# Chunk-selected attention and a squared-ReLU layer on one core: the last two sequences score two heads at once, and the chunk selection becomes a mask spread by DMA

## The chip, the cores and the metric

The kernel runs on one core of a Trainium2 chip. A core has five engines with instruction streams of their own: TensorE (PE in the profile; its weight loads are listed as PEld), VectorE (DVE), ScalarE (ACT), GpSimd (POOL) and SyncE (SP, which here only issues DMAs). They meet through semaphores. Data lies in SBUF (128 partitions), matmuls write to PSUM (eight banks of 512 floats per partition), and 16 DMA engines move data to and from DRAM. The metric is the device time of one execution in microseconds.

## The reference

Four sequences of 768 positions, eight heads of 64 dimensions. Keys are cut into 24 chunks of 32. For each query, an upper bound of its score against each chunk is worked out from the chunk's smallest and largest key; the six chunks with the highest bound are kept, future chunks being barred, and the query attends to the earlier positions of the kept chunks alone. The result goes through a layer with a squared ReLU.

```python
k_min, k_max = k_chunks.min(axis=3), k_chunks.max(axis=3)
ub = sum(maximum(q * k_min, q * k_max), axis=-1)        # 24 bounds a query
ub = where(pos // 32 >= chunk, ub, -1e9)
top_chunks = argsort(ub)[..., -6:]
scores = where(chunk_of_j in top_chunks and j <= i, q @ k.T / 8, -1e9)
attn = exp(scores - max) / (sum(...) + 1e-9)
x = (attn @ v) reordered to [3072, 512]
out = (relu(x @ w_in) ** 2) @ w_out                     # 512 -> 2048 -> 512
```

## The kernel before, in words

Work is cut into 16 head pairs (four a sequence, `p` from 0 to 15; `hh` is the head in the pair). The first 128 positions of each sequence see at most four chunks and are treated apart (`first_attention`, line 566); the rest is five query tiles of 128 positions per head.

For each pair, `stage_a` (line 622) prepares the operands. Keys and queries of sequences 0 and 1 are turned on TensorE; those of sequences 2 and 3 (`BY_DMA = 2`) come already turned from DMA transposes on SP's queue (tiles `kt`, `qt`, two heads on 2 x 64 partitions). VectorE reduces each chunk to its maximum and minimum (line 697), TensorE makes the bounds (660, 662), VectorE adds the bar on future chunks (722), finds the eight highest (668) and marks the chunks that are not among the six (727). The marks are turned (on TensorE, or for sequences 2 and 3 by DMA, line 389) and copied below the queries as 24 more rows (682). Keys are copied likewise above 24 rows of -32768 at the chunk's own columns (694, 336). So one matmul over 64 + 24 = 88 rows gives a score and takes 32768 off wherever the chunk is not chosen: nothing else has to know the selection.

`stage_b` (766) makes, for each head, five PSUM banks of four 128x128 score tiles (`BANKS`, 748; line 782), the exponential of each bank on ScalarE (804), the triangle on the diagonal tiles on VectorE or GpSimd (`causal`, 756), and the products with the values (793). VectorE divides by the sums (612, 614). `ffn` (823) turns the result by DMA or TensorE and runs the up-projection (866), ReLU (873, 875), square (884) and down-projection (897), one call for the first tiles and one for each sequence.

The order is not that of the code. Every piece is an operation with engines and costs, a due time, needs and buffers; `Plan.order` (115) simulates the engines and DMA queues once on the host and takes, on the engine that can start first, the operation with the earliest due time. The instructions are then written in that fixed order. The dictionary `P` (240) holds the due times' parameters. Buffers are slots by tag: three PSUM banks "ps", one "tp", two "av", two "ff"; six "e" tiles for exponentials; six "kq" tiles for natural or turned keys and queries. Loads are DMAs on GpSimd's queue (all of them in a fixed order), output stores and DMA transposes go through SP's queue.

## Time and profile before

| what | value |
|---|---|
| median of 3 runs | 266.53 us (265.86 to 267.04) |
| profiled execution, span from first to last instruction | 263.6 us |
| TensorE busy | 251.4 us, 95% |
| ScalarE busy | 197.8 us, 75% |
| VectorE busy | 183.0 us, 69% |
| GpSimd busy | 106.4 us, 40% |
| score matmuls (line 782) | 51.7 us busy, 320 instructions |
| exponentials (line 804) | 86.4 us busy, 160 instructions |
| DMA | 26.51 MB, mean 101 GB/s |

The page has a row of 40 equal slices per engine, each digit the busy tenths of 6.6 us. Groups of instructions are listed as "line engine operation output<-input shape xcount | busy us, mean ns of one | idle before, and what ended it". Matmuls are pipelined: one has a duration of some 0.2 us, but the next can start long before it ends, so the pace is read from start to start.

### The profile page before, as it was taken

How to read it: one execution, taken by the hardware profiler on the slowest of the kernel's cores; microseconds unless marked ns; L12 is line 12 of the kernel's file. 1: busy time of each engine (PE TensorE's matmuls, PEld its weight loads, DVE VectorE, ACT ScalarE, POOL GpSimd, SP SyncE). 2: the span in 40 equal slices, each digit the busy share in tenths (PEclk: the TensorE clock that was granted, in tenths of full speed). 3: DMA queues.
4: the chain of work that ended last, by engine and by line, in shares of the span. 5: the costliest groups of instructions: out<-in, count | busy, mean ns of one | idle time of the engine just before them, and what ended most of it. 6: DMA issues, size and time to landing. Idle time of an engine off the chain costs nothing.

```text
span 263.6 us, 6555 instructions
## 1 busy us (share of the span) xinstructions
PE 251.4 (95%) x2382; PEld 164.1 (62%) x2405; DVE 183.0 (69%) x663; ACT 197.8 (75%) x395; POOL 106.4 (40%) x185
## 2 busy tenths in 40 slices
PE   6899999999999999999999999998999999999995
PEld 1577566666687666665686645666865564765443
DVE  7569999778999999998999943644757142455000
ACT  6658897859899999999989845987866692677111
POOL 7998987799555599833311201110200010000000
PEclk9799999999999999999999999999999999999999
DMA  8999999999999999995440001154000113400122
GB/s 153 156 175 180 181 198 190 94 126 174 170 151 166 149 157 143 123 145 148 87 93 15 2 20 75 44 82 101 2 0 15 42 44 99 120 2 0 40 82 80
DMA packets 106336, 26.51 MB, mean 101 GB/s; under 512 B 99008, under 2 KB 103360, under 8 KB 106304
## 3 DMA queue, kind: packets, MB, share of 16 engines
q0 software_dynamic: 75088, 13.11, 67.9%
q1 hardware_dynamic: 31216, 12.98, 24.0%
q8 instruction: 19, 0.31, 0.5%
q14 instruction: 13, 0.11, 0.2%
HBM read 27.26 MB, written 6.29 MB: 127 GB/s over the span
## 4 chain that ended last, share of the span: by engine, by line
PE 62%; DVE 24%; ACT 8%; issue 3%; DMA 2%; SPq 0%; ACTq 0%; DVEq 0%
PE py L897 25%; PE ph L866 20%; PE ps L782 8%; PE av L793 4%; DVE h L884 4%; DVE kr L697 4%; DVE m L668 3%; DVE qsc L283 3%; ACT e L804 2%; DMA xT<-x 2%; ACT ht L873 2%; DVE x L614 2%; ACT qsc L281 2%; DVE kqc L283 1%; DVE ubm L722 1%
## 5 line engine op out<-in xcount | busy, mean ns | idle before, releaser
L866 PE MATMUL ph<-xT,w_in_sb 128*128 128x256 bf16 (+2 forms) x592 | 95.7, 304 | 1.6 <-DMA xT<-x 1.2
L804 ACT ACTIVATE e<-ps 128x512 bf16<-128x512 f32 x160 | 86.4, 608 | 7.5 <-PE ps L782 4.4
L897 PE MATMUL py<-w_out_sb,h 128*128 128x512 bf16 (+2 forms) x377 | 87.9, 370 | 1.2
L762 POOL TENSOR_SCALAR_AFFINE_SELECT e<-e 128x128 bf16<-128x128 bf16 (+1 forms) x88 | 31.0, 365 | 101.0 <-ACT e L804 89.1
L866 PEld LDWEIGHTS <-w_in_sb 128*128 128x128 bf16 x592 | 55.6, 97 | 24.9 <-DMA xT<-x 1.6
L873 ACT ACTIVATE ht<-ph 128x384 bf16<-128x384 f32 (+2 forms) x130 | 58.9, 457 | 16.2 <-PE ph L866 12.5
L884 DVE TENSOR_TENSOR h<-ht 128x256 bf16<-128x256 bf16 (+2 forms) x148 | 47.8, 333 | 16.4 <-ACT ht L873 12.9
L897 PEld LDWEIGHTS <-h 128*128 128x128 bf16 x400 | 36.2, 97 | 33.8
L782 PE MATMUL ps<-qsc,kqc 88*128 88x128 bf16 (+1 forms) x320 | 51.7, 272 | 0.3 <-DVE ubm L722 0.2
L782 PEld LDWEIGHTS <-kqc 88*128 88x128 bf16 x320 | 27.6, 97 | 14.8 <-issue 0.8
L281 ACT COPY ob<-py 128x512 f32<-128x512 f32 (+2 forms) x22 | 12.5, 570 | 29.2 <-PE py L897 29.1
L793 PEld LDWEIGHTS <-e 128*128 128x128 bf16 x640 | 29.6, 97 | 6.4 <-issue 0.3
L793 PE MATMUL av<-vn,e 128*128 128x65 bf16 x480 | 29.6, 193 | 0.0
L759 DVE TENSOR_TENSOR e<-e,tri 128x128 bf16<-128x128 bf16 (+1 forms) x40 | 9.7, 242 | 14.9 <-ACT e L804 14.2
L614 DVE TENSOR_TENSOR x<-av,rc 128x320 bf16<-128x320 f32 (+1 forms) x40 | 18.7, 472 | 0.5
L668 DVE MAX8 m<-ubm 128x8 f32<-128x24 f32 x160 | 15.5, 167 | 0.0
L697 DVE TENSOR_REDUCE kr<-kT 128x24 bf16<-128x768 bf16 x16 | 14.8, 951 | 0.2
L697 DVE TENSOR_REDUCE kr<-kt 128x24 bf16<-128x768 bf16 x16 | 14.8, 935 | 0.0
L793 PE MATMUL av<-v,e 128*128 128x65 bf16 x160 | 13.9, 193 | 0.1
L875 DVE TENSOR_SCALAR ht<-ph 128x256 bf16<-128x256 f32 (+2 forms) x18 | 8.2, 454 | 8.2 <-PE ph L866 8.2
L612 DVE RECIPROCAL rc<-av 128x5 f32<-128x5 f32 (+1 forms) x40 | 7.2, 184 | 9.4 <-PE av L793 8.5
L281 ACT COPY qsc<-sT 24x256 bf16<-24x256 bf16 (+1 forms) x29 | 12.4, 427 | 1.6 <-DMA sT<-selb 0.9
(92 smaller groups left out, 258.7 us busy)
## 6 DMA issues: line engine op xcount, KB each, us to landing
out_dram<-ob SPq DMA_DIRECT2D x23, 256.0 KB, 2.2
w_in_sb<-in_moe_w_in_dram POOLq DMA_DIRECT2D x4, 512.0 KB, 7.2
w_out_sb<-in_moe_w_out_dram POOLq DMA_DIRECT2D x4, 512.0 KB, 8.8
vn<-in_v_dram POOLq DMA_DIRECT2D x15, 128.0 KB, 6.9
nt<-in_k_dram POOLq DMA_DIRECT2D x10, 128.0 KB, 6.6
nt<-in_q_dram POOLq DMA_DIRECT2D x10, 128.0 KB, 5.3
kn<-in_k_dram POOLq DMA_DIRECT2D x8, 80.0 KB, 7.0
qn<-in_q_dram POOLq DMA_DIRECT2D x8, 80.0 KB, 5.7
```

The lines of the kernel that those rows point to most:

```text
L281: nc.scalar.copy(dst, src)
L614: return plan.op({"DVE": 0.06 + 0.00108 * D * n}, due, lambda _: nc.vector.tensor_mul(x(), av[:, :, 0:D], rc[:, 0:n].unsqueeze(2).to_broad ...
L668: nc.vector.max(out=m8[:, i, hh], in_=ubm[:, i, hh])
L697: nc.vector.tensor_reduce(kr[:, mm].rearrange("d (t c) -> d t c", c=128 // CH) if b >= BY_DMA else kr[:, mm], part(kT).rearrange("d t (c j ...
L762: nc.gpsimd.affine_select(out=e, in_=e, compare_op=ALU.is_ge, fill=0.0, base=0, channel_multiplier=-1, pattern=[[0, n], [1, 128]])
L782: nc.tensor.matmul(ps[:, 128 * c:128 * (c + nt)], lhsT=kqs[:, s, hh, 128 * j:128 * (j + 1)], rhs=qss[:, s, hh, 128 * (t0 - 1):128 * (t0 - ...
L793: nc.tensor.matmul(av[:, t - 1], lhsT=e[:, 128 * c:128 * (c + 1)], rhs=value_tile(b, h, j), start=(i == 0 and c == 0), stop=(i == len(BANK ...
L804: nc.scalar.activation(e.tile, ps.tile, ACT.Exp, scale=scale), [sc], [ps, e])
L866: nc.tensor.matmul(ph.tile, lhsT=w_in_sb[:, ki, 128 * f:128 * (f + 1)], rhs=xT[:, c0 // 128:c1 // 128, ki], start=(ki == 0), stop=(ki == N ...
L873: nc.scalar.activation(ht.tile, ph.tile, ACT.Relu)
L884: {"DVE": 0.067 + w / 1920}, at[0] + P["h2"], lambda _: nc.vector.tensor_mul(h2[f][:, c0:c1], ht.tile, ht.tile), [op], [ht, h2[f]])))
L897: nc.tensor.matmul(py.tile, lhsT=h2[f][:, 128 * t:128 * (t + 1)], rhs=w_out_sb[:, f, c0:c1], start=(f == 0), stop=(f == NFI - 1))
```

## The change

Sequences 0 and 1 stay as they are, in `stage_a` and `stage_b`. For sequences 2 and 3 two new functions take over.

`stage_a_turned` makes bounds and the eight highest as before, then marks the chosen chunks (four comparisons, only for chunks up to the tile's own), multiplies the marks by 3e38, turns them by a DMA transpose and stores them to a DRAM tile `seen`. Four DMAs on GpSimd's queue then read `seen` so that each row, 512 bytes for both heads of the pair, lands in the 32 partitions of its chunk: a tile `mask` of 128 partitions x 21 key-and-query tiles x 2 heads x 128 queries. GpSimd zeroes the triangle in the five diagonal tiles of the mask. No 88-row operands are built: the copies of keys, queries and marks are gone for these sequences.

`score_banks` computes the scores from the turned keys and queries themselves: for each 128x128 tile, a matmul of head 0 on rows 0 to 63 and one of head 1 on rows 64 to 127, by turns, into two banks. Two such steps, four banks (three "ps" and "tp"), make one operation. `stage_b_turned` takes the exponential, then the minimum with the mask on VectorE (0 where a key is not seen, 3e38 where it is), then the values.

The masks share a tag "set" of three slots with the 88-row sets of sequences 0 and 1 (two slots) and the natural keys and queries of sequence 1 (one). "e" goes from six to eight, "kq" from six to four; the bounds of these sequences go to "ff". The planner gets a cost `SWITCH` when TensorE passes between operations of 128 and of 64 rows, and all parameters in `P` are new, among them 59 single shifts of due times.

```diff
+    SWITCH = 0.095
...
+                if op.rows != rows:
+                    cost += self.SWITCH
+                rows = op.rows
...
-    P = dict(lead=[0, 207.45, 109.14, 153.29, -29.2, 112.12, 38.49, 53.35, 112.23, 30.95,
...
-             sel=2, loads='Q3 K3 V0 V1 Q2 K2 i0 V2 k0 V3 q0 i1 k1 v2 q1 i2 '
...
+    P = dict(lead=[-41.26, 277.74, 117.47, 192.23, -33.04, 156.27, 37.46, 53.28,
...
+             h2=-5.788, later='q1 k1 v1 k2 v3 q2 k3 v2 q3', shift={1035: 18.86, 381:
...
+             xt=(1, 2, 3), ub='ff', tp=1, vm2=4.275, va2=52.931,
...
-    plan = Plan({"tp": 1, "ps": 3, "av": 2, "ff": 2, "e": 6, "h2": NFI + 6, "ht": 3,
-                 "ob": 3, "kq": 6, "nt": 6,
+    plan = Plan({"tp": 1, "ps": 3, "av": 2, "ff": 2, "e": 8, "h2": NFI + 6, "ht": 3,
+                 "ob": 3, "kq": 4, "nt": 6, "set": 3, "seen": 3,
...
-    kqs = consts.tile([KC, NSET, 2, S], BF16, tag="kqs", name="kqc")
-    qss = consts.tile([KC, NSET, 2, QC], BF16, tag="qss", name="qsc")
+    sets = [buffer("set", [128, 2, 2, S + QC], name="kqc") for _ in range(2)]
+
+    def kqs(rows, s, *cols):
+        return sets[s // 2][(rows, s % 2, *cols, slice(0, S))]
+
+    def qss(rows, s, *cols):
+        return sets[s // 2][(rows, s % 2, *cols, slice(S, S + QC))]
...
+        both = buffer("set", [128, 2, NS, H, D], name="kqn")
         for nm in "kq":
-            if b < BY_DMA:
+            if b == BY_DMA - 1:
+                nat[nm, b] = both
...
+    UNITS = [(t, j) for t in range(1, NT) for j in range(t + 1)]
+    NU = len(UNITS)
+    FIRST = [UNITS.index((t, 0)) for t in range(1, NT)]
+    BIG = 3.0e38
+    NM = NU + 1
+    NB = NU // 4
+    PLACE = {(t, j): j + (0, 0, 3, 6, 10, 15)[t] for t, j in UNITS}
+    masks = {}
+    written = []
+
+    def stage_a_turned(p):
+        b, hp = divmod(p, NP)
+        s = p % NSET
+        t0 = HALVES * p - P["lead"][p]
+        op = plan.op
+        kT, qT = turned["k", b], turned["q", b]
+        qp, qm = buffer("qp", [128, QC]), buffer("qm", [128, QC])
+        ub = buffer(P["ub"], [128, NS, 2, NC], F32, name="ub")
+        sT = buffer("st", [128, 2, 128], name="sT")
+        seen = buffer("seen", [2 * 128, 128], name="seen")
+        mask = masks[p] = buffer("set", [128, NM, 2, 128], name="mask")
+
+        def like(t):
+            return t.rearrange("d (t u j) -> d u t j", u=2, j=64)
+
+        kb = chunk_bounds(
+            p, t0, list(loaded["k", b]), kT, lambda t: t[:, :, hp],
+            lambda t: t.rearrange("d t (c j) -> d t c j", j=CH),
+            lambda t: t.rearrange("d (t c) -> d t c", c=128 // CH))
+        sq = halves(qp, qm, lambda: qT[:, :, hp].rearrange("d t (u j) -> d u t j", u=2),
+                    like, list(loaded["q", b]), qT, t0, 0.34)
+        ubm, m8, m = ranked(p, t0, sq, kb, qp, qm, ub)
+        chosen = selbs[:, s].rearrange("p t h c -> p (t h c)")[:, 0:2 * 128]
+
+        def select(i0, i1):
+            n = 4 * (i1 + 1)
+            c0 = 8 * PLACE[i0 + 1, 0]
+            nc.vector.tensor_tensor(
+                chosen[:, c0:c0 + 2 * n * (i1 - i0)].rearrange(
+                    "p (i c h) -> p i h c", h=2, c=n), ubm[:, i0:i1, :, 0:n],
+                m8[:, i0:i1, :, TOPK - 1:TOPK].to_broadcast([128, i1 - i0, 2, n]),
+                op=ALU.is_ge)
+
+        def pick(*runs):
+            for r in runs:
+                select(*r)
+
+        def enlarge():
+            nc.vector.tensor_single_scalar(chosen[:, 0:8 * NM], chosen[:, 0:8 * NM], BIG,
+                                           op=ALU.mult)
+
+        sel = [op({"DVE": 0.23}, t0 + 19, lambda _: pick((0, 2), (2, 3)),
+                  m[:1] + prepared.get((p - NSET, "sT"), []), [ubm, m8])]
+        sel = [op({"DVE": 0.37}, t0 + 19, lambda _: (pick((3, 4), (4, 5)), enlarge()),
+                  m + sel, [ubm, m8])]
+        t = turn_by_dma(lambda: sT.tile, lambda: chosen, t0 + 21, sel, [sT],
+                        640, -0.8)
+        prepared[p, "sT"] = [t]
+        w = op({"SP": 0.45}, t0 + 23, lambda _: nc.sync.dma_start(
+            out=seen.tile.rearrange("(x r) j -> r x j", r=128), in_=sT.tile),
+            [t] + written[-1:], [sT, seen, mask], packets=300, turns=True, late=1.0)
+        written.append(w)
+
+        def spread_rows(g):
+            rows = seen[0:8 * NM].rearrange("(u g h) j -> g u (h j)", g=4, h=2)
+            nc.gpsimd.dma_start(
+                out=mask[32 * g:32 * g + 32].rearrange("c u h j -> c u (h j)"),
+                in_=rows[g].unsqueeze(0).to_broadcast([32, NM, 2 * 128]))
+
+        spread = [op({"POOL": 0.86}, t0 + 25 + g, lambda _, g=g: spread_rows(g),
+                     [w], [seen, mask], packets=1850, free=True, late=0.2)
+                  for g in range(4)]
+        for i in range(NB):
+            u = [PLACE[x] for x in UNITS[4 * i:4 * i + 4] if x[0] == x[1]][0]
+            prepared[p, "mask", i] = [op(
+                {"POOL": 0.37}, t0 + 30 + i, lambda _, u=u: causal("POOL", mask[:, u], 2),
+                spread, [mask])]
...
+    bursts = {}
+
+    def bank(p, hh, i):
+        return bursts[p, hh, i]
+
+    def score_banks(todo, due):
+
+        def go(_):
+            for p, i in todo:
+                b, hp = divmod(p, NP)
+                kT, qT = turned["k", b], turned["q", b]
+                for c, (t, j) in enumerate(UNITS[4 * i:4 * i + 4]):
+                    for hh in range(2):
+                        rows = slice(D * hh, D * hh + D)
+                        nc.tensor.matmul(bank(p, hh, i)[:, 128 * c:128 * (c + 1)],
+                                         lhsT=kT[rows, j, hp], rhs=qT[rows, t - 1, hp],
+                                         start=True, stop=True)
+
+        for n, (p, i) in enumerate(todo):
+            for hh in range(2):
+                bursts[p, hh, i] = buffer("tp" if n and hh else "ps", [128, 512], F32,
+                                          name="ps")
+        seqs = sorted({p // NP for p, _ in todo})
+        sc = plan.op({"PE": 0.225 * len(todo)}, due, go,
+                     [o for b in seqs for nm in "kq" for o in loaded[nm, b]]
+                     + scored_last[-1:],
+                     [bank(p, hh, i) for p, i in todo for hh in range(2)]
+                     + [turned[nm, b] for b in seqs for nm in "kq"], rows=64)
+        scored_last.append(sc)
+        for n, (p, i) in enumerate(todo):
+            for hh in range(2):
+                stage_b_turned(p, hh, i, sc, due + 4 * n + 2 * hh)
+
+    sums = {}
+    scored_last = []
+
+    def stage_b_turned(p, hh, i, sc, due):
+        b, hp = divmod(p, NP)
+        h = 2 * hp + hh
+        ps = bank(p, hh, i)
+        e = buffer("e", [128, 512])
+        if i == 0:
+            sums[p, hh] = buffer("av", [128, NS, D + 1], F32), None
+        av, prev = sums[p, hh]
+
+        def values(_):
+            for c, (t, j) in enumerate(UNITS[4 * i:4 * i + 4]):
+                nc.tensor.matmul(av[:, t - 1], lhsT=e[:, 128 * c:128 * (c + 1)],
+                                 rhs=value_tile(b, h, j),
+                                 start=(i == 0 and c == 0), stop=(i == NB - 1),
+                                 skip_group_check=True)
+
+        done = plan.op({"ACT": 0.48}, due + 0.5, lambda _: nc.scalar.activation(
+            e.tile, ps.tile, ACT.Exp, scale=scale), [sc], [ps, e])
+        u = PLACE[UNITS[4 * i]]
+        def choose(_):
+            seen = masks[p][:, u:u + (4 if i else 6), hh]
+            like = e.tile.rearrange("p (u j) -> p u j", j=128)
+            if not i:
+                seen = seen.rearrange("p (a b) j -> p a b j", b=3)[:, :, 0:2]
+                like = like.rearrange("p (a b) j -> p a b j", b=2)
+            nc.vector.tensor_tensor(like, like, seen, op=ALU.min)
+
+        done = plan.op({"DVE": 0.39}, due + P["vm2"], choose,
+            [done] + prepared[p, "mask", i], [e, masks[p]])
+        prev = plan.op({"PE": 0.125}, due + P["va2"], values,
+                       [done, prev, made["ones", b]] + loads_of("v", b, hp),
+                       [e, av, nat["v", b]])
+        sums[p, hh] = av, prev
+        if i == NB - 1:
+            x = inputs[b]
+            x_done[b, 1].append(normalise(
+                av, NS, lambda: x[:, :, D * h:D * (h + 1)], prev, [x], due + 7))
...
+    inputs = {b: buffer("x", [128, NS, d_model]) for b in range(B)}
     for b in range(B):
-        x = buffer("x", [128, NS, d_model])
+        x = inputs[b]
         x_done[b, 1] = []
         for p in range(NP * b, NP * (b + 1)):
-            stage_a(p)
-            stage_b(p, x)
+            if b < BY_DMA:
+                stage_a(p)
+                stage_b(p, x)
+            else:
+                stage_a_turned(p)
+        if b == BY_DMA - 1:
+            for c in range(BY_DMA, B):
+                x_done[c, 1] = []
+        if b >= BY_DMA:
+            todo = [(p, i) for p in range(NP * b, NP * (b + 1)) for i in range(NB)]
+            for n in range(0, len(todo), 2):
+                score_banks(todo[n:n + 2], HALVES * NP * b + 4 * n)
```

211 lines of the change are left out of this document (103 added, 108 removed), and 9 rows, old and new, of the table h2.

## The prediction

> **What bounds the kernel now.** I read the engine totals, the 40 slices and the chain of waits first. The first number of a slice row is busy tenths.
>
> ```profile
> span 263.6 us, 6555 instructions
> PE 251.4 (95%) x2382; PEld 164.1 (62%) x2405; DVE 183.0 (69%) x663; ACT 197.8 (75%) x395; POOL 106.4 (40%) x185
> ...
> PE   6899999999999999999999999998999999999995
> DVE  7569999778999999998999943644757142455000
> ...
> DMA  8999999999999999995440001154000113400122
> ...
> PE 62%; DVE 24%; ACT 8%; issue 3%; DMA 2%; SPq 0%; ACTq 0%; DVEq 0%
> ```
>
> TensorE (PE) is busy 95% of the span, its slices are 9 from the second on, and the chain that ended last is TensorE for 62%. No other engine is above 75%. The DMA engines are full up to slice 19 (19 x 6.6 = 125 us) and have room behind it. Then I cut the span where the work changes: the start, sequences 0 and 1, the part from 115 us that holds the attention of the last two sequences, and the last feed-forward.
>
> ```profile
> core 0: us, PE busy (x) PEld busy (x) DVE busy (x) ACT busy (x) POOL busy (x), PEclk, DMA share, GB/s
> 0.00:20.00 20.00, 15.95 (x155) 10.19 (x156) 12.89 (x49) 12.63 (x22) 18.17 (x30) 0.91 1.63 162
> 20.00:115.00 95.00, 92.04 (x1000) 62.79 (x1007) 89.62 (x314) 84.33 (x166) 74.75 (x117) 1.00 1.89 159
> 115.00:225.00 110.00, 108.12 (x1010) 69.69 (x1021) 69.68 (x270) 83.55 (x172) 13.52 (x39) 1.00 0.24 56
> 225.00:263.60 38.60, 35.29 (x226) 21.41 (x225) 10.82 (x33) 17.27 (x38) 0.00 (x0) 1.00 0.15 51
> ```
>
> Between 20 and 225 us TensorE is idle 2.96 + 1.88 = 4.8 us of 205, at a granted clock of 1.00: these stretches are as long as their matmuls. Their end moves only if TensorE gets less to do, or is made to wait. VectorE (DVE) has 94% in the second stretch and 63% in the third. The profiled execution spans 263.6 us; the median of the runs is 266.53, so 2.9 us lie around the span. I sum against the span and add 2.9.
>
> **The change, part by part: TensorE.** The scores of sequences 2 and 3 are 16 heads x 5 banks of 512 columns = 80 banks. What one costs today is in the chain and in the group of line 782:
>
> ```profile
> 163.83 0.66 PE ps L782 x6
> ```
> ```profile
> L782 PE MATMUL ps<-qsc,kqc x320: 216/272/327, 29.4 to 216.8; 88*128 88x128 bf16 x128, 88*128 88x256 bf16 x32
> ```
>
> Six matmuls are three banks (two runs a bank), so a bank is 0.66 / 3 = 0.22 us and 80 are 17.6 us. After the change the same columns run as pairs of 64-row matmuls, one head on the upper and one on the lower half of the rows. The trace holds this form: the first-tile attention, line 583, eight matmuls, two heads by turns. Matmuls first, then weight loads:
>
> ```profile
> 15.08 0.40 PE L286 MATMUL xt<-ident,x 128*128 128x128 bf16 x4
> 15.41 0.40 PE L583 MATMUL ps<-t,t 64*128 64x128 bf16 x8
> 15.74 0.94 PE L539 MATMUL ph<-warm 128*128 128x256 bf16 x7
> ```
> ```profile
> 15.07 0.23 PEld L286 LDWEIGHTS <-x 128*128 128x128 bf16 x4 [0.46 <-DVE x L614]
> 15.40 0.23 PEld L583 LDWEIGHTS <-t 64*128 64x128 bf16 x8
> 15.73 0.77 PEld L539 LDWEIGHTS <-warm 128*128 128x128 bf16 x8
> ```
>
> The eight matmuls last 0.40 us together. The last alone lasts 0.21 (the least of line 782's row, 216 ns), so eight starts are spread over 0.19, that is 27 ns each, or 0.217 for eight, which is two banks. A bank of four whole-row tiles at 0.22 us is 55 ns for 128 columns. So two row halves do run side by side: 80 banks become 40 x 0.217 = 8.7 us.
>
> Against this stands the change of form. Line 583's loads end at 15.40 + 0.23 = 15.63 and the next whole-row load begins only at 15.73, 0.10 later; in the matmul rows the start at 15.41 comes 0.33 after 15.08, where four matmuls take 4 x 0.055 = 0.22, so 0.11 are lost going in; coming out, 15.74 is 0.33 after 15.41, where eight take 0.217, so another 0.11. The page TensorEngine Tiling (Array Packing) of the Trainium skill, section Key Properties, says that changing the tiling mode drains TensorE; by that rule there is a loss at each change, and the trace agrees with 0.11. Four banks (16 matmuls) go in one group, so there are 20 groups with two changes each: 20 x 2 x 0.11 = 4.4 us. The bounds are 0 (all three gaps might be other waits) and 2 x 20 x 0.13 = 5.2 (a time stamp's rounding on each side). I take 4.4, the row itself. TensorE's sum: -17.6 + 8.7 + 4.4 = **-4.5 us**. Values, bounds and feed-forward matmuls stay as they are.
>
> **ScalarE, VectorE, GpSimd.** The rows that price the removed copies and the added minimum:
>
> ```profile
> L804 ACT ACTIVATE e<-ps 128x512 bf16<-128x512 f32 x160 | 86.4, 608 | 7.5 <-PE ps L782 4.4 <-PE av L793 2.0 <-POOL e L762 0.4
> ...
> L884 DVE TENSOR_TENSOR h<-ht 128x256 bf16<-128x256 bf16 x72 | 20.4, 294 | 7.9 <-ACT ht L873 4.9
> ...
> L281 ACT COPY kqc<-kt 64x768 bf16<-64x768 bf16 x9 | 7.4, 827 | 0.1
> ...
> L281 ACT COPY qsc<-qt 64x640 bf16<-64x640 bf16 x7 | 5.1, 724 | 0.2
> ...
> L884 DVE TENSOR_TENSOR h<-ht 128x512 bf16<-128x512 bf16 x12 | 5.1, 429 | 0.0
> ...
> L283 DVE COPY qsc<-qt 64x640 bf16<-64x640 bf16 x9 | 2.9, 327 | 0.1
> ...
> L283 DVE COPY kqc<-kt 64x768 bf16<-64x768 bf16 x7 | 2.6, 379 | 0.1
> ...
> L875 DVE TENSOR_SCALAR ht<-ph 128x512 bf16<-128x512 f32 x2 | 1.3, 664 | 0.0
> ```
> ```profile
> L283 DVE COPY qsc<-sT x35: 219/289/442, 28.1 to 203.1; 24x384 bf16<-24x384 bf16 x19, 24x256 bf16<-24x256 bf16 x16
> L281 ACT COPY qsc<-sT x29: 362/401/509, 37.0 to 203.2; 24x256 bf16<-24x256 bf16 x16, 24x384 bf16<-24x384 bf16 x13
> ```
> ```profile
> L762 POOL TENSOR_SCALAR_AFFINE_SELECT e<-e x88: 287/324/881, 31.2 to 214.4; 128x128 bf16<-128x128 bf16 x68, 128x256 bf16<-128x256 bf16 x20
> ```
> ```profile
> 115.00:225.00 110.00, 7.00 (x29) 1.00 0.24 56
> ```
>
> For eight head pairs the copies that built the 88-row operands go. ScalarE loses 7.4 + 5.1 and half of the 29 selection copies, 14.5 x 0.401 = 5.8: -18.3 us, worth nothing by itself, since TensorE is what lasts. VectorE loses 2.6 + 2.9, 17.5 x 0.289 = 5.1, and the triangle multiplications of this stretch, 7.0: -17.6 us. It gains 80 minima of 128x512. The trace has no minimum; the nearest is the two-operand bf16 row of the same shape, 429 ns. From below, the growth from 256 to 512 columns is 135 ns, so 512 columns back to back may cost 270; from above, the one 128x512 with float input took 664. I take 429: +34.3 us. The selection becomes four comparisons and one multiplication for one comparison: four more instructions a pair, none above the 294 of the 256-column row, 8 x 4 x 0.294 = 9.4. Net 34.3 + 9.4 - 17.6 = +26.1, which puts the third stretch at 69.7 + 26.1 = 95.8 of 110 - 4.5 = 105.5 us, 91%. The second stretch ran at 94% with TensorE idle 2.96 of 95, so I cost this at nothing; the cover is thin (third rival).
> GpSimd loses the triangle on scores in this part and makes it once on each mask: 5 selects a pair, 40 in all, up to 0.41 each as two-tile forms, 16.4 us. It is busy 13.5 of 110 there, so this is free unless it waits.
>
> **The mask's way.** For each pair: transpose by DMA (as before, smaller), a store of 64 KB to DRAM on SP's queue, four spreads on GpSimd's queue, five selects on GpSimd, then the minima.
>
> ```profile
> DMA packets 106336, 26.51 MB, mean 101 GB/s; under 512 B 99008, under 2 KB 103360, under 8 KB 106304
> ...
> q0 software_dynamic: 75088, 13.11, 67.9%
> ...
> L866 PE MATMUL ph<-xT,w_in_sb 128*128 128x256 bf16 (+2 forms) x592 | 95.7, 304 | 1.6 <-DMA xT<-x 1.2
> ```
> ```profile
> L447 POOL DMA_DIRECT2D vn<-in_v_dram x15 | 13.4, 924 | 0.0
> ```
> ```profile
> out_dram<-ob SPq DMA_DIRECT2D x23, 256.0 KB, 2.2
> ...
> sT<-selb SPq DMA_TRANSPOSE x8, 2.3
> ```
>
> The transpose lands in 2.3 us and stays. The store is new on SP: 8 issues, each waiting for its transpose, with output stores and the transposes of x for the feed-forward queued behind; a landing is 2.2 us (the nearest store, four times larger), so a transpose of x may come some 2.3 us later. All that TensorE waited for these transposes in the whole run is in the row of line 866, 1.2 us, because matmuls of other work stand ready when x is due; so this costs between 0 and 2 x 2.3 for the two sequences, and I take 0, the nearer end. The spreads add 32 issues at 0.92 = 29.6 us to GpSimd's queue, which is open after 115 us. What waits behind a blocked issue there are the last loads and the selects. Their bytes: 32 partitions x 21 rows x 512 B x 4 = 1.38 MB a pair, 11.0 MB in 21,504 packets. By packets: queue 0's 75,088 took 67.9% of 16 x 263.6, so 38 ns each; 21,504 x 0.038 / 16 = 51 us of the full DMA side. By bytes at the mean of 101 GB/s: 109 us. The share in the third stretch is 0.24, so 84 of 110 us are free: 51 fits, 109 does not. I take 51, since nearly all of queue 0's packets are below 512 B and packets, not bytes, seem to set its time. Then each mask takes 6.4 us and three buffers are enough. Cost on the path: nothing, by cover of the feed-forward matmuls.
> Buffers: one tag of three slots holds first the key and query sets of sequences 0 and 1 and sequence 1's natural keys and queries, then the masks. The first masks need sequence 1's last transposes. The bounds' PSUM tile moves to the feed-forward's two banks; the four score banks are taken together and come free after four exponentials.
>
> **The refit** changes the order everywhere. It can at best remove TensorE's idle time ahead of 225 us, 4.05 + 2.96 + 1.88 = 8.9; it can add as much as it likes. No row prices it: taken as 0.
>
> **Sum:** 263.6 - 4.5 = 259.1 us span, + 2.9 = **262.0 us**, 1.7% below the median.
>
> **The rivals.**
> (1) *The change of form is hidden, or the refit removes idle time:* 17.6 - 8.7 = 8.9 saved, 257.6 us. For it: the only rows of the form lie in the busy first 16 us, where other waits may stand in the gap. Against: the gap shows on both sides.
> (2) *Masks late, slower:* place: GpSimd's spreads from 115 us to the last scores, today at 216.8. It decides when eight masks take longer than 216.8 - 4.5 - 115 = 97 us, 12.1 us a mask or 114 GB/s. At 101 GB/s they take 109, 12 us too long, 274; at 108 the gain is gone. Middle 270. For it: the trace's mean rate, and DMA engines full until 125 us, so the first mask competes with the last loads. Against: the packet count.
> (3) *VectorE takes the pace from 115 us on, no change:* at the 94% it has held, the stretch has room for 0.94 x 105.5 = 99 us; without the minima it holds 61.5, so it decides from (99 - 61.5) / 80 = 0.47 us a minimum, and at 0.52 all 4.5 us are gone: 266.5. For it: 0.429 is close. Worse, if each of the 40 selects on GpSimd held up one minimum for its 0.41, a minimum would cost 0.429 + 0.205 = 0.63 on average, the stretch 112 us of VectorE, at 94% 119, and the run 263.6 + 9 + 2.9 = 276. Against that: line 762's row has a median of 324 ns and only its maximum, 881, looks like such a wait, though VectorE was over 90% busy beside most of them. I give it 0.02. The page SBUF — State Buffer of the Trainium skill, section SBUF: two separate sides, says that the two lock each other out for whole instructions, when the VectorE operation has two SBUF inputs and the GpSimd one reads SBUF; the row's median does not bear it out.
>
> **How the numbers follow.** The forecast 0.50, rival 1 0.12, rival 2 0.24, rival 3 0.14. About 0.5%, 1.3 us, is what a measurement can tell from no change. Faster: 0.48 of the forecast, rival 1, 0.02 of rival 3 = 0.62. Same: 0.02 + 0.08 of rival 3 = 0.10. Slower: rival 2 and 0.04 of rival 3 = 0.28. The range 257.5 to 271 leaves out half of rival 1 (0.06) and half of rival 2 (0.12). The likeliest case by itself is 260 to 264.5: a minimum between 270 and 470 ns, a change of form between 0.05 and 0.12, and one or two lost microseconds.
>
> **What would show it.** Right: the new scores' matmuls come every 27 ns within a group, gaps of 0.1 us at both ends, TensorE's total about 4 us lower with slices still 9; a minimum near 0.43 us; VectorE near 90% from 115 to 220 us; masks landed before the exponentials they cut. Wrong: TensorE idle over 3 us in the third stretch behind a VectorE minimum (then ask whether it waited for a mask or for its own queue), matmuls of the row halves 55 ns apart, or the last feed-forward beginning later than 221 us.

## The result and the profile after

The changed kernel takes **277.68 us** (median of 4 runs, 276.97 to 278.34) beside 266.25 for the kernel before in the same session: a ratio of 1.0437 [1.0393, 1.0481]. I had forecast 262.0, faster. It is 4.4% slower, and the time lies above the range's upper end of 271. The page of the kernel after, cut to the lines that are used:

```profile
span 276.6 us, 6954 instructions
PE 253.3 (92%) x2548; PEld 159.3 (58%) x2548; DVE 195.4 (71%) x707; ACT 184.7 (67%) x373; POOL 132.8 (48%) x219
...
PE   7888999999999999994699799659999999999995
...
PEclk9999999999999999999799999997999999999999
DMA  8999999999999999999985997959999115300022
...
q0 software_dynamic: 78672, 24.12, 88.0%
...
L981 DVE TENSOR_TENSOR e<-e,mask 128x512 bf16<-128x512 bf16 x80 | 33.6, 443 | 13.1 <-ACT e L972 6.6
...
L825 POOL DMA_DIRECT2D mask<-seen x32 | 22.6, 713 | 33.7 <-PE ph L1037 12.5
L857 POOL TENSOR_SCALAR_AFFINE_SELECT mask<-mask 128x256 bf16<-128x256 bf16 x40 | 17.0, 460 | 30.5 <-DMA mask<-seen 30.5
...
mask<-seen POOLq DMA_DIRECT2D x32, 336.0 KB, 8.6
```

The profiled execution spans 276.6 us, 13.0 more than before and 17.5 more than my 259.1. TensorE's row of 9s has holes at slices 19 and 20 and at slices 23, 26 and 27; the granted clock has a 7 at slices 20 and 28, behind two of them. The DMA row, which before was 5 and below from slice 19 on, is mostly 9 as far as slice 31. Two of the stretches that were read before:

```profile
core 0: us, PE busy (x) PEld busy (x) DVE busy (x) ACT busy (x) POOL busy (x), PEclk, DMA share, GB/s
20.00:115.00 95.00, 92.60 (x1010) 61.78 (x1011) 88.84 (x316) 82.30 (x163) 74.57 (x116) 1.00 1.90 158
115.00:225.00 110.00, 96.22 (x1098) 59.93 (x1096) 80.79 (x304) 69.10 (x147) 40.25 (x74) 0.97 0.85 149
```

Up to 115 us little has changed. In the stretch from 115 us TensorE was busy 108.12 us of 110 before and is busy 96.22 now: 11.9 us more of idle time, and a clock of 0.97 that is worth some 3 us more. These are about 15 of the 17.5 us; the DMA share there has gone from 0.24 to 0.85. TensorE's two longest waits (us in total, times, longest) are for the transposes of x and for a minimum:

```profile
PE ph L1037 <- DMA xT<-x: 5.8, 1, 5.8
PE av L967 <- DVE e L981: 4.6, 2, 3.7
```

The chain of waits says what stood behind them (start, duration, what):

```profile
122.72 10.62 DMA xT<-x
...
153.21 9.33 DMA mask<-seen
...
169.64 9.24 DMA sT<-selb
178.89 3.78 DMA seen<-sT
```

The transposes of x of sequence 1 hold the end up for 10.62 us; for the first half of it TensorE had other work, then it stood for 5.75. A mask takes 9.33 us from GpSimd's queue to its select, a transpose of marks 9.24 and its store another 3.78.

The second stall ends with a minimum at 186.53 us. The mask that it needed had landed by 181.30 us, but its selects stood on GpSimd's queue behind the issue of the next spreads, and that issue waited for the late transpose and its store (start, duration, what, then idle time and its cause):

```profile
183.24 2.83 POOL L825 DMA_DIRECT2D mask<-seen  x4 [8.03 <-DMA seen<-sT]
186.07 2.22 POOL L857 TENSOR_SCALAR_AFFINE_SELECT mask<-mask 128x256 bf16<-128x256 bf16 x5
```

A landing is the time from a transfer's issue to its arrival. The least, median and longest landing of the transposes of x, after and then before:

```profile
DMA to landing us min/median/max: 2.4/5.1/11.5
```
```profile
DMA to landing us min/median/max: 2.4/2.5/5.2
```

So one transfer that is the same in both kernels takes twice as long at the median and up to 11.5 us. The five of the last sequence, issued from 228 us when the spreads are over, land after 2.4 to 2.5 again; the ten before take 3.7 to 11.5. Windows of after around the stalls, with the same columns as above, show a second price:

```profile
120.00:135.00 15.00, 9.25 (x79) 4.85 (x79) 7.51 (x26) 4.11 (x8) 1.84 (x5) 0.93 1.23 151
150.00:160.00 10.00, 8.55 (x81) 4.75 (x75) 8.45 (x30) 6.29 (x14) 7.75 (x13) 1.00 0.77 131
170.00:180.00 10.00, 7.89 (x117) 4.62 (x114) 6.94 (x31) 5.78 (x12) 5.05 (x9) 1.00 0.89 173
180.00:190.00 10.00, 6.25 (x71) 3.45 (x69) 4.88 (x14) 4.88 (x10) 5.05 (x9) 0.87 0.68 141
```

The long stalls (5.75 us of idle TensorE ending at 133.5 us, and 3.75 ending at 187.2) bring a lower clock, 0.93 and 0.87 in these windows; 1.45 us of idle time in the window from 150 and 2.11 in that from 170 leave it at 1.00. The page TensorE: Matmul & The Clock Gate of the Trainium skill, section Why this matters for your kernels, warns of idle gaps over some 3 us between matmuls; the trace agrees in these two places, but in two runs below an idle time of 2.87 us and one of 2.63 lost the clock too, so the limit that was measured here is lower.

Times of the experiments are medians of undisturbed executions; of the last two experiments three executions in four were disturbed, 3 to 4% longer with long half-clock stretches, and only such ones were profiled, so that the stalls in their profiles are compared with each other alone.

### The profile page after: what moved, and what is told of

It is laid out like the page before. It is cut to its first block, busy times and chain, and to the rows that moved or that the text cites. A ratio compares the mean times of both kernels' runs of the same rounds, so it can differ in the third digit from the quotient of the medians.

```text
span 276.6 us, 6954 instructions
## 1 busy us (share of the span) xinstructions
PE 253.3 (92%) x2548; PEld 159.3 (58%) x2548; DVE 195.4 (71%) x707; ACT 184.7 (67%) x373; POOL 132.8 (48%) x219
## 3 DMA queue, kind: packets, MB, share of 16 engines
q0 software_dynamic: 78672, 24.12, 88.0%
## 4 chain that ended last, share of the span: by engine, by line
PE 57%; DVE 17%; DMA 15%; POOL 6%; ACT 2%; issue 2%; POOLq 0%; SPq 0%; DVEq 0%; ACTq 0%
PE ph L1037 23%; PE py L1068 19%; DVE kr L675 5%; PE ps L877 4%; DMA xT<-x 4%; DMA mask<-seen 3%; DMA sT<-selb 3%; DMA v<-in_v_dram 3%; PE av L967 3%; PE ps L934 2%; PE av L889 2%; DVE m L660 2%; DVE h L1055 2%; DVE x L649 2%; POOL mask L825 2%
## 5 line engine op out<-in xcount | busy, mean ns | idle before, releaser
L1068 PE MATMUL py<-w_out_sb,h 128*128 128x512 bf16 (+2 forms) x400 | 92.0, 373 | 0.4 <-DVE ubm L689 0.4
L1044 ACT ACTIVATE ht<-ph 128x384 bf16<-128x384 f32 (+2 forms) x122 | 55.4, 459 | 22.3 <-PE ph L1037 18.5
L981 DVE TENSOR_TENSOR e<-e,mask 128x512 bf16<-128x512 bf16 x80 | 33.6, 443 | 13.1 <-ACT e L972 6.6
L302 ACT COPY ob<-py 128x512 f32<-128x512 f32 (+2 forms) x25 | 14.2, 569 | 41.4 <-PE py L1068 41.3
L825 POOL DMA_DIRECT2D mask<-seen x32 | 22.6, 713 | 33.7 <-PE ph L1037 12.5
L857 POOL TENSOR_SCALAR_AFFINE_SELECT mask<-mask 128x256 bf16<-128x256 bf16 x40 | 17.0, 460 | 30.5 <-DMA mask<-seen 30.5
L877 PE MATMUL ps<-kqc 88*128 88x384 bf16 (+2 forms) x160 | 26.1, 272 | 0.1
L857 POOL TENSOR_SCALAR_AFFINE_SELECT e<-e 128x128 bf16<-128x128 bf16 (+1 forms) x50 | 17.8, 367 | 14.6 <-ACT e L901 12.5
L1046 DVE TENSOR_SCALAR ht<-ph 128x256 bf16<-128x256 f32 (+2 forms) x26 | 12.1, 473 | 11.5 <-PE ph L1037 11.3
L967 PE MATMUL av<-vn,e 128*128 128x65 bf16 x240 | 17.1, 195 | 0.0
L877 PEld LDWEIGHTS <-kqc 88*128 88x128 bf16 x160 | 13.2, 97 | 6.8 <-issue 0.8
L889 PE MATMUL av<-vn,e 128*128 128x65 bf16 x240 | 15.8, 193 | 0.0
```

Of the source, the lines that this page charges most:

```text
L825: nc.gpsimd.dma_start(out=mask[32 * g:32 * g + 32].rearrange("c u h j -> c u (h j)"), in_=rows[g].unsqueeze(0).to_broadcast([32, NM, 2 * 1 ...
L857: nc.gpsimd.affine_select(out=e, in_=e, compare_op=ALU.is_ge, fill=0.0, base=0, channel_multiplier=-1, pattern=[[0, n], [1, 128]])
L877: nc.tensor.matmul(ps[:, 128 * c:128 * (c + nt)], lhsT=kqs(slice(0, KC), s, hh)[:, 128 * j:128 * (j + 1)], rhs=qss(slice(0, KC), s, hh)[:, ...
L889: nc.tensor.matmul(av[:, t - 1], lhsT=e[:, 128 * c:128 * (c + 1)], rhs=value_tile(b, h, j), start=(i == 0 and c == 0), stop=(i == len(BANK ...
L967: nc.tensor.matmul(av[:, t - 1], lhsT=e[:, 128 * c:128 * (c + 1)], rhs=value_tile(b, h, j), start=(i == 0 and c == 0), stop=(i == NB - 1), ...
L981: nc.vector.tensor_tensor(like, like, seen, op=ALU.min)
```

## The experiments

**Theory after the result.** The spreads keep the 16 DMA engines full from 115 us on; the small transfers that stand between two pieces of work then land late (transposes of x after 3.7 to 11.5 us and transposes of marks after 4.8 to 12.8, in place of some 2.5; stores of marks after 3.3 at the median, one after 12.5); TensorE runs out of work and loses clock besides. **Rivals:** VectorE with its minima is the pace; the row halves or their changes of form cost more than I counted; the spread's 512-byte rows are at fault, not its bytes. The kernel before was measured again with each group of experiments, with medians of 266.04, 265.46, 265.96, 265.27 and 265.34; each ratio is against its own.

**A mask of 6 rows in 21.** The spreads bring 29% of the bytes; all else stays. The kernel leaves out the other 15 rows of the mask.

```diff
-                out=mask[32 * g:32 * g + 32].rearrange("c u h j -> c u (h j)"),
-                in_=rows[g].unsqueeze(0).to_broadcast([32, NM, 2 * 128]))
+                out=mask[32 * g:32 * g + 32, 0:6].rearrange("c u h j -> c u (h j)"),
+                in_=rows[g][0:6].unsqueeze(0).to_broadcast([32, 6, 2 * 128]))
...
-        u = PLACE[UNITS[4 * i]]
+        u = 0
```

> The changed kernel in its own order, but each of the 32 spreads brings only 6 of its 21 rows, and every minimum and every triangle on the mask uses those first rows: the same operations, waits and order, 29% of the spread bytes; the mask is then not the right one. Theory A (the spreads keep the DMA engines busy, so that SP's transposes and stores land late and TensorE waits for them): transposes of x land in about 3 us instead of 5 to 11, TensorE loses under 4 us from 115 us on, and the run takes 262 to 266 us, the forecast. Theory B (the minima on VectorE, or the written order with its waits, are what lasts, not the bytes): above 273 us.

Measured: 265.49 us, 0.9976 [0.9942, 1.0011] of before. The stretch from 115 us and the landings of x:

```profile
115.00:225.00 110.00, 106.71 (x1160) 64.91 (x1174) 83.67 (x315) 72.29 (x151) 37.44 (x75) 1.00 0.40 94
```
```profile
DMA to landing us min/median/max: 2.4/2.5/4.1
```

With the same operations in the same order 12.2 us are gone, TensorE is idle 3.29 us of the stretch in place of 13.78, its clock is 1.00, and the transposes of x land in 2.5 at the median again. The spreads' traffic causes the loss. VectorE as the pace is out: its 80 minima are still there. The run doesn't divide the loss between small transfers that were held up and masks that were late themselves (a spread landed after 8.6 us at the median, here after 3.2).

**One row in 21**, spread over all minima by a broadcast on the reading side.

```diff
+                out=mask[32 * g:32 * g + 32, 0:1].rearrange("c u h j -> c u (h j)"),
+                in_=rows[g][0:1].unsqueeze(0).to_broadcast([32, 1, 2 * 128]))
...
+            seen = masks[p][:, 0:1, hh].to_broadcast([128, 4, 128])
```

> As the run with 6 of 21 rows, with one row: 5% of the spread bytes; each minimum reads that row four times over. The run with 29% of the bytes took 265.5 us against 266.0 before, 3.5 more than the forecast of 262. If the rest of the traffic still holds transposes up, this run takes 262 to 264; if the saving on TensorE is smaller than summed, or the new order loses it elsewhere, it stays at 265 to 266.

265.45 us, 0.9979 [0.995, 1.0008]: nothing more is to be had below 6 rows. Even with the traffic all but gone the change gains about 0.5 us by the ratio, which isn't clear of nothing, and not the 4.5 of my TensorE sum.

**Only the first mask thin.** As the 6-row mask, but for pair 8 alone.

```diff
+        few = 6 if p == 8 else NM
```

> The changed kernel with all spreads whole but those of the first mask (pair 8), which bring 6 of 21 rows. Those are the ones in flight when the transposes of sequence 1's x are issued, and TensorE stood 5.75 us waiting for them, with 1.7 us more at half clock afterwards. If that collision is the cause of that stall: the stall at 128 us goes and the run takes 269 to 272 us. If the transposes are late for another reason (SP's queue, the last loads), the stall stays and the run takes 276 or more.

271.12 us, 1.0184 [1.0132, 1.0235], so 6.6 us come back of the 11.4 lost. The chain and the transposes of x:

```profile
144.06 10.79 DMA sT<-selb
154.87 8.28 DMA seen<-sT
```
```profile
DMA to landing us min/median/max: 2.4/2.5/6.8
```

The chain no longer waits for x; it waits later, for marks and their store, 10.79 and 8.28 us. So the largest piece of the loss lies where the first mask's spreads (issued at 116.5 us) meet the transposes of x of sequence 1 (issued from 121.4).

**Traffic alone, on the kernel before.** 32 DMAs of the spreads' size and rows into a buffer nobody reads.

```diff
+                    for g in range(4):
+                        plan.op({"POOL": 0.72}, due + g, lambda _, g=g, mask=mask:
+                                nc.gpsimd.dma_start(
+                                    out=mask[32 * g:32 * g + 32],
+                                    in_=moe_w_out[21 * g:21 * g + 21, 0:128].unsqueeze(
+                                        0).to_broadcast([32, 21, 128])),
+                                [sc], [mask])
```

> The kernel before, with 32 spreads of the changed kernel's size and form (32 partitions x 21 rows of 512 bytes from DRAM) that nobody reads, four behind a score of each of the eight last pairs; they wait for nothing but that score and their buffer, 4 buffers instead of 6 for keys and queries. The run before with stores and spreads took 297 us, but there GpSimd's queue stood still behind waiting spreads and held up the triangles. Theory A: traffic alone makes transposes late here too, 268 to 276 us. If it costs under 2 us, the changed kernel's loss is in the mask's chain of waits, not in other transfers.

291.19 us, 1.0937 [1.0884, 1.0989]. The stretch from 115 us, TensorE's two longest waits and the landings of x:

```profile
115.00:225.00 110.00, 92.81 (x828) 59.94 (x832) 65.56 (x247) 71.32 (x143) 31.69 (x63) 0.91 0.84 130
```
```profile
PE ph L876 <- DMA xT<-x: 9.3, 2, 6.1
PE ps L782 <- DVE qsc L283: 4.5, 1, 4.5
```
```profile
DMA to landing us min/median/max: 2.4/8.1/12.9
```

Nothing in this kernel reads what these DMAs bring, and TensorE is busy 92.81 of 110 us in place of 108.12, at a clock of 0.91. The transposes of x land after 8.1 us at the median. TensorE's longest waits are for transposes of x, 9.3 us, and for a copy of marks (`qsc`, line 283), 4.5 us, itself behind a transpose of marks; none of its longer waits is for GpSimd. The loss of 25 us is larger than the change's own: the old order has its transposes at other places, and GpSimd's queue waits for the one buffer too (24.7 us in all), so the amount isn't transferable; the sign and the mechanism are.

An earlier form of this test hung the real store and spreads on the old kernel.

> The kernel before, with the store of the marks and the four spreads of 344 KB added for each of the eight last pairs; nobody reads what they bring (one buffer for it, four instead of six for keys and queries, which leaves the order as it was). Theory A: the traffic alone makes the transposes land late and costs this kernel 4 to 12 us, 270 to 278. Theory B (traffic is harmless, the wait is for the masks): within 2 us of the kernel before.

296.88 us, 1.1134 [1.1047, 1.1221]. It doesn't separate the causes: GpSimd's queue stood behind the single buffer (22.9 us), the triangles of the scores stood behind the queue, and TensorE waited 14.2 us for them.

**The row halves.** The 6-row kernel with score matmuls over all 128 rows: no pairs, no change of form.

```diff
-                        rows = slice(D * hh, D * hh + D)
+                        rows = slice(0, 128)
```

> As the run with 6 of 21 rows, but each score matmul takes all 128 rows of keys and queries instead of one head's 64 (both heads' sums, so the scores are not the right ones): the same number of matmuls, no two side by side, and no change of form. By the sum of the prediction TensorE has 17.1 - 8.6 = 8.5 us more to do and 20 x 2 x 0.11 = 4.4 less to wait, 4.1 in all: 269 to 270 us against 265.5. If the row halves bring nothing in the end, or TensorE is not the bound, under 267.

268.73 us, 1.0104 [1.0073, 1.0135], 3.2 us more than the 6-row kernel where my sum gives 4.1. The score group of the 6-row kernel and then of this one:

```profile
L934 PE MATMUL ps<-qt,kt 64*128 64x128 bf16 x320 | 12.4, 218 | 0.0
```
```profile
L934 PE MATMUL ps<-qt,kt 128*128 128x128 bf16 x320 | 21.1, 219 | 0.0
```

12.4 against 21.1 us busy: 8.7 less for the halves, and 8.7 - 3.2 = 5.5 of it given back around them, near the 4.4 I had set for the changes of form. Read from the starts of the matmuls, a group with a change on each side is 0.23 us shorter than the same group here, 4.7 us for all 20. But this kernel, without halves, takes 3.3 us more than the kernel before (265.46, measured beside it), where the sum has half a microsecond less for it: something else in the new kernel costs time, traffic aside. A second try, all four tiles of head 0 before head 1's, was to take the pairing away.

```diff
-                for c, (t, j) in enumerate(UNITS[4 * i:4 * i + 4]):
-                    for hh in range(2):
+                for hh in range(2):
+                    for c, (t, j) in enumerate(UNITS[4 * i:4 * i + 4]):
```

> As the run with 6 of 21 rows, but in each group all four tiles of head 0 are scored before the four of head 1, so that no two neighbouring matmuls use different row halves. If the halves run side by side only by turns, the 40 pairs of banks take 17.1 instead of 8.6 us, and if TensorE bounds the run, the time rises by 7 to 9 us over that run; if something else bounds it, by under 3.

265.6 us, 0.9973 [0.993, 1.0016]: no change. It didn't take the pairing away: matmuls still start every 28 ns on average within a group, where the 6-row kernel has 27. So this run says nothing on what the pairing is worth.

**Rows or bytes.** First the mask's rows 528 bytes apart in SBUF, meant to keep each 512-byte row a packet of its own.

```diff
-        mask = masks[p] = buffer("set", [128, NM, 2, 128], name="mask")
+        mask = masks[p] = buffer("set", [128, NM, 2 * 128 + 8], name="mask")
```

> All rows and bytes as in the changed kernel, but the mask's rows in SBUF stand 528 bytes apart instead of 512, so that neighbouring rows cannot be joined into one packet of 4096 bytes. Theory A1 (a 256-byte packet of a transpose stands behind a 4096-byte packet of a spread, which takes about 0.36 us, each time, because the engines serve the queues packet by packet): packets of 512 bytes, transposes land in 3 to 6 us, the run takes 264 to 270 us. Theory A2 (it is the bytes in all that fill the DMA engines, whatever their packets): the spreads take as long or longer, the transposes stay late, 277 us or more.

279.2 us, 1.0505 [1.0414, 1.0596]. Queue 0 has the same 78,672 packets as after, so nothing was split and the run is inconclusive. Then the opposite: the marks are stored (by four small stores in place of one) so that every mask partition reads one run of 10,752 bytes.

```diff
-            rows = seen[0:8 * NM].rearrange("(u g h) j -> g u (h j)", g=4, h=2)
+            row = seen[g].rearrange("u h j -> (u h j)")
...
-                in_=rows[g].unsqueeze(0).to_broadcast([32, NM, 2 * 128]))
+                in_=row.unsqueeze(0).to_broadcast([32, NM * 2 * 128]))
```

> The changed kernel, with the marks stored in DRAM in another order (by four smaller stores a pair on SP's queue instead of one), so that each partition of the mask is one run of 10,752 bytes in DRAM instead of 21 rows of 512; same bytes, same order, same result. In the changed kernel a packet of eight 512-byte rows holds a DMA engine for 0.36 us, 45 ns a row, and queue 0's time rose by 64 us of the full DMA side. If it is the rows that cost, the masks take under 40 us of it, transposes land earlier and the run takes 267 to 274 us. If it is the bytes, queue 0's time stays and the run takes 276 or more (four stores instead of one may add a little).

281.8 us, 1.0611 [1.0516, 1.0707], beside 1.0437 for the change as it is: slower, not faster. Page and chain:

```profile
q0 software_dynamic: 76624, 24.12, 82.5%
...
mask<-seen POOLq DMA_DIRECT2D x32, 336.0 KB, 6.3
```
```profile
130.41 6.89 DMA xT<-x
...
144.50 9.26 DMA sT<-selb
```

A spread lands after 6.3 us in place of 8.6, and queue 0's time falls from 88.0% of 276.6 = 243 us to 82.5% of 280.1 = 231. The transposes beside it still take 6.89 and 9.26. So long rows make the spreads cheaper, and the small transfers are held up all the same. The edit also makes 32 stores of marks out of 8, and GpSimd's issues wait 19.4 us for them in all (12.3 after), so the slower time can't be put down to the rows. The unread traffic on the kernel before in this form:

> The kernel before with the 32 spreads that nobody reads, as in the run that took 291 us, but each partition reads one run of 10,752 bytes instead of 21 rows of 512. If rows cost: 270 to 282 us. If bytes cost: 288 to 294.

280.4 us, 1.0534 [1.0437, 1.0632], 10.8 us less than with 512-byte rows. Here, with no store added, the long rows did help. I keep from the two only that neither row length made the traffic free.

**The whole kernel with the first mask held back.** In a first run the four spreads of pair 8 were given the transposes of x of sequence 1 as a need in the plan.

```diff
-                     [w], [seen, mask], packets=1850, free=True, late=0.2)
+                     [w] + (xt_all[-1] if p == 8 else []), [seen, mask], packets=1850,
+                     free=True, late=0.2)
```

> The changed kernel with all its work, but the four spreads of the first mask (pair 8) are issued only when the five transposes of x of sequence 1 have landed. Theory (the spreads' traffic holds up the transposes, and the first place is sequence 1's x): the stall of 5.75 us before the feed-forward's first matmul of sequence 1 goes to under 1.5 us, those transposes land within 5 us, the later stalls stay or grow by 1 to 2 us, since pairs 8 and 9 are now spread back to back; 270 to 274 us. Rival (the first mask is needed early, so that holding it back moves the wait to a minimum of pair 8): TensorE waits over 4 us for a minimum that waits for mask 8, 276 us or more. If neither the transposes nor the time change, the collision at this place is not with pair 8's spreads: 277 to 279.

It held nothing back: a need in the plan sets the order within each queue, and GpSimd's queue had no other work, so the spreads still went out at 115.4 us. What was left was another order. It took 282.05 us (265.27 before); the stall before x was 8.1 us. In the second run a small copy on GpSimd, from the transposed x into the mask, stands ahead of the spreads.

```diff
+            held = [op({"POOL": 0.1}, t0 + 24, lambda _: nc.gpsimd.tensor_copy(
+                mask[:, 0, 0, 0:4], xT1[:, NS - 1, 0, 0:4]), made + [w], [mask, xT1])]
```

> The changed kernel with all its work. Making the first mask's spreads wait in the plan alone changed only the order of the queues: on the chip they still went out at 115.4 us, ahead of the transposes of x of sequence 1. Here a small copy on GpSimd, from the last transposed x into the mask, stands ahead of the four spreads, so they really go out only when the transposes have landed (about 125 us); otherwise the queues' order is that of the run before this. Theory (traffic of the spreads holds up the transposes): the stall ahead of sequence 1's feed-forward goes from 8.1 us to under 2, its transposes land within 5 us; the spreads of pairs 8 and 9 then collide with what comes next, so 3 to 7 us are won against the run before this, undisturbed runs compared. Rival (the first mask is needed at once): a minimum of pair 8 waits for over 4 us, and nothing is won. If the transposes land as late as before with no spread under way, the theory falls at this place.

283.7 us (265.34 before): nothing is seen to be won against the run before it. The chain:

```profile
124.47 2.74 DMA xT<-x
...
133.34 13.59 DMA sT<-selb
146.94 5.78 DMA seen<-sT
...
193.54 14.57 DMA xT<-x
```

Now that the spreads wait for it, x lands after 2.74 us in place of 10.06, and the stall there is down from 8.1 to 1.1 us. The two masks that were held back, eight spreads at once, then meet a transpose of marks: 13.59 us for it and 5.78 for its store, and TensorE stands 11.22 us behind a minimum. The next x, unprotected, takes 14.57. The collision was moved, not removed. The theory's mechanism shows on the full kernel, with both outcomes in one trace; the gain of 3 to 7 us that I expected didn't come.

## Why the prediction was wrong, step by step

The miss is 277.68 - 262.0 = 15.7 us. The spreads' traffic makes 12.2 of it (277.68 against 265.49 with 29% of their bytes); 3.5 are left without it.

*What bounds the kernel.* Right: TensorE, and with little slack to give. That was also the warning I didn't use: a kernel idle for 4.8 us of 205 has little to put in place of work that waits for a late transfer.

*TensorE.* The two terms were right. Starts within a group are 27 to 28 ns apart on average (27 forecast); read from start to start a change of form costs 98 ns going in and 122 coming out (110). The page TensorEngine Tiling (Array Packing) of the Trainium skill, section Key Properties, says that a change of mode drains TensorE; the trace agrees. Against the whole-row kernel the gain was 3.2 us (4.1 by the sum). But the changed kernel with its traffic all but gone is at 265.5, not 262.0, and counted in spans none of the 4.5 us arrived: 263.8 us with 6 rows (264.0 before), 263.8 with one row (263.4 before). The 2.9 us that I added around the span were a median of the runs less the span of one execution; the executions of the experiments have 2.0 to 2.2 us there in the kernel before and about 1.7 in those built on the change. Since the whole-row kernel has the loss too, it isn't in the halves. It is in something that the sum had at nothing, the new order or the waits for masks; no run separates these, and the cause of the 3.5 us stays open. The lower clock of the first 20 us in the profiles (0.83 in the 6-row kernel, 0.91 before) isn't it: among 22 executions of the 6-row and one-row kernels, 6 had a clock of 0.998 or more over the whole span and took 265.6 us on average, the other 16 took 265.5.

*ScalarE, VectorE, GpSimd.* Cost nothing that a run shows, as I took it. A minimum took 0.443 us (0.429), a select 0.460 (0.41 as the upper end), a spread's issue 0.713 (0.92). VectorE's total rose by 12.4 us (26.1): the minima are right, and I had the copies and comparisons wrong by some 13 us, so that VectorE was busy 73% of the stretch from 115 us and not about 90. Rival 3 isn't borne out as the pace, but its lock shows. The least, median and longest of the minima, in ns:

```profile
L981 DVE TENSOR_TENSOR e<-e,mask x80: 386/419/622, 139.0 to 225.9; 128x512 bf16<-128x512 bf16 x80
```

Of the 80 minima, 68 overlap no select and take 0.39 to 0.43 us. Eleven were issued while a select ran: they take 0.52 to 0.62 and end 0.28 to 0.29 us after that select's end, as if their work had begun only then. The rule of SBUF — State Buffer in the Trainium skill, section SBUF: two separate sides, beside which I had said minima might take 0.63, is borne out for these eleven. I had rejected it by the median of a row; it costs VectorE some 2 us in all, because few minima meet a select, and no run shows that TensorE paid for it.

*The mask's way: the step that failed.* I wrote "Cost on the path: nothing, by cover of the feed-forward matmuls", and of the store and the transposes of x "this costs between 0 and 2 x 2.3 [...] and I take 0, the nearer end". The store and the transposes were priced with landings of 2.2 and 2.3 us, medians that come mostly from a stretch in which the DMA engines were a quarter busy, and the change itself takes that quiet away. The runs showed landings up to 11.5 us for x and 12.8 for marks, 11.9 us more of idle TensorE, and 12.2 us back when most of the bytes are taken away. The trace of before held a sign of it: two of its eight transposes of marks, issued at 108 and 110 us while the loads still filled the DMA engines, landed after 4.9 and 4.8 us in place of 2.3. I had also named the selects among what waits behind a blocked issue on GpSimd's queue, and set no price on it; the second stall is such a wait. I had asked whether the mean share leaves room (84 of 110 us free) and not what a transfer of 2.3 us costs while a burst is in the engines. The page DMA: Bandwidth & Descriptors of the Trainium skill, section Issuing engines are not separate DMA queues, says that DMAs of SP and GpSimd run on the same 16 engines and interleave; the trace agrees (transposes from SP land late while GpSimd's spreads are under way), and I had not drawn on it.

The load was mis-sized as well. (The DMA engines were also full only to the end of slice 18, 119 us, and not to 125 as I read; their 19th digit is a 5.) Queue 0 holds 78,672 - 75,088 = 3,584 packets more, not 21,504: eight rows of 512 bytes travel as one packet. Its time rose by 88.0% of 276.6 less 67.9% of 263.6, 64.4 us of the full side where I had 51: far fewer packets than I counted, each far longer. This alone would still have fitted the 84 us that I counted as free.

*The rivals.* Rival 2 had the direction, the place (GpSimd's spreads from 115 us) and nearly the time (270 to 274). Its condition was wrong: eight masks were to take longer than 97 us, 12.1 each, and a spread landed after 8.6 at the median. What decides is less the masks' rate than what is caught behind them. The sign that I had named for being wrong, TensorE idle over 3 us behind a minimum, came only as the second-largest stall (3.75 us); I had named none for the transposes of x. The other sign came too: the last feed-forward begins at 238.5 us (225.5 before), not by 221. Rival 1 can't have been the case: the change of form shows, and idle time grew.

*The refit.* Taken as 0. Up to 115 us that holds: TensorE is busy 92.60 of 95 us, before 92.04. Behind it the order decides which transfers collide: two other orders of the same work, the last two runs, were at 282 and 284. The 3.5 us that are left without the traffic may be the order's too; that isn't shown.

## What to carry to other kernels

A burst of DMA that is hidden by its own deadline isn't free: list the small transfers that are issued while it is under way and sit on the path, and price those at the landing time beside the burst (here 4 to 13 us for a transpose in place of some 2.5), not at their quiet one. A mean DMA share says whether the bytes fit, not who waits. And moving a burst away from one victim only helps when no other stands behind it, so the first remedy to look for is fewer bytes: at 29% of them, in a kernel that leaves out most of the mask, the traffic's loss was gone.

## What the runs showed of the hardware beside this

- Eight 512-byte rows of a broadcast travel as one packet: in the trace's DMA records most packets of the spreads have 4,096 bytes and take 361 ns at the median, those of the transposes 256 bytes and 18 ns. One run of 10,752 bytes a partition travels as a packet of that size.
- Two heads' matmuls on row halves run side by side even when the four of one head are issued ahead of the other's four: 27 to 28 ns from start to start both ways.
- A TensorE idle time of 3.75 us was followed by a stretch at half clock of 3.4 us, 1.7 us lost; the idle times of 0.6 to 2.0 us were not. In the run with only the first mask thin 2.87 us, and in the one with long rows 2.63 us, brought such a stretch as well, while 2.35 us in each of these runs did not.
- A VectorE minimum of two SBUF tiles that is issued while a GpSimd select runs ends some 0.28 us after the select: 0.52 to 0.62 us in place of 0.42, in eleven cases of eleven.
